# A convolution kernel's reload in four transfers in place of two, one store on ScalarE's queue, and a new order of the work

## The chip, the cores and the metric

The kernel runs on one core of a Trainium2 chip. The metric is the device time of one execution in microseconds (us), the median of several; the profiler records one execution by itself, and its span is the time from the first to the last recorded instruction of that execution. TensorE (PE in the profile) does the matmuls, its weight loads are listed apart (PEld), VectorE is DVE, ScalarE is ACT, GpSimd is POOL, and SyncE (SP) issues DMA transfers. SPq, ACTq and POOLq are the queues by which an engine issues transfers.

## The reference, cut to what matters

x is one sequence of L = 2048 tokens by D = 512 channels in bf16. It is normalised over the channels, and two layers work on the result xn, an S4 convolution with N = 128 modes for each channel, and a gated layer with F = 1792:

```python
P = exp(dt * A)[:, :, None] ** l            # 512 channels, 128 modes, 2048 lags
K = einsum("dn,dnl,dn->dl", C, P, dt * B).real
y = irfft(rfft(pad(xn)) * rfft(pad(K))) + xn * Dskip      # causal convolution over 2048 tokens
h = sigmoid(xn @ w_gate) * (xn @ w_up)
out = x + y + h @ w_down
```

## The kernel before, in words

The kernel is a list of 930 operations, put on the list by `pl.add` and `pl.copy` (lines 258 to 299), each with its engine, what it depends on, and the buffers that it takes and gives back. The table `ORDER` (line 207) is a permutation of that list; `run` (line 291) walks along it, hands out buffers by it, and issues each operation on its engine. An engine does its operations in that order and waits where an operation isn't ready. So the table alone sets what stands behind what on every engine and queue; there are no due times.

There are four strands of work.

- LayerNorm (lines 529 to 590): statistics on VectorE (L542, L543), the square root on POOL (L481, L482), the reciprocal (L501) and the scaling on VectorE (L554) or ScalarE, for groups of four tiles of 128 tokens. The normalised tokens go to memory and come back transposed (`xnT`, L581).
- The convolution's kernel. For four blocks c of 128 columns, VectorE raises powers of the modes step by step (L736, L737, L741, L742) with help of ScalarE (L790), into two tables G and H. TensorE multiplies these in two halves of 64 small matmuls on 128x32 tiles (`f_k`, L821). ScalarE evicts each half to `kq_sb` (L288), two stores of 96 KB bring the block to `k_scr` in memory (the helper `dma`, whose transfers are all recorded as L422), and a reload brings two blocks of it back in another layout, as `kT[pc]` with pc = c // 2. Before, one reload of 384 KB does that for a pair of blocks, behind the four stores of both. Then VectorE adds the skip factor Dskip to one row of it (`f_ds`, L842), and POOL copies one value of that row (L844).
- The convolution itself, in two halves p of the channels (p = 0 uses `kT[0]`, blocks 0 and 1; p = 1 uses `kT[1]`, blocks 2 and 3), with eight units u in each half. A unit has: a load of `z_scr` (256 KB); `fm`, four or more small matmuls on 64x64 tiles (L883); the eviction of their result to x (ScalarE, L288); a swap of 32-row groups of x, by four transfers of 64 KB on SP for p = 0 and for units 4, 6 and 7 of p = 1, by four copies of VectorE (L896) for units 0, 1, 2, 3 and 5 of p = 1; `fk`, ten matmuls of `kT[p]` with a constant E (L909), which need `f_ds`; the eviction of that (ScalarE, L288); two products on VectorE (L914, L918), which need both the swap and the eviction; `fv`, sixteen small matmuls on 64x64 tiles (L933); its eviction (ScalarE) and a store of 256 KB to `v_scr`. At the end the result is loaded again, and TensorE brings it back to tokens (L992, L995).
- The gated layer, in four groups (grp) of 512 tokens, with 14 pieces k of F: gate (L1043) and up (L1067) matmuls of 128x128 weights with 512 tokens, a sigmoid on ScalarE (L1055), a copy of up on ScalarE (L1082) and a product on VectorE (L1087), or a product straight from PSUM (L1092); then down (L1121). These matmuls are what fills TensorE between the pieces of the convolution.

TensorE's full matmuls (L909, L1043, L1067, L1121) use the whole 128x128 array; fm, fv and `f_k` cut it in tiles. A run of such matmuls between full ones is called a visit to small tiles below.

The lines that the change touches are the block's end (lines 831 to 844) and `ORDER`.

Of the kernel before, what the change touches and what calls it, by code (L numbers as in the profile page):

```python
# [13 lines left out]
ACT = mybir.ActivationFunctionType  # L14
# [53 lines left out]
KB = 1024  # L68
# [114 lines left out]
def _consts():  # L183
# [135 lines left out]
def kernel(  # L319
# [336 lines left out]
    W_op = []  # L656
# [63 lines left out]
    kT_op = [[], []]  # L720
    k_st = [[], []]
# [26 lines left out]
    for c in range(4):  # L748
# [83 lines left out]
        kq_free = [dma("SP", k_scr[4 * c:4 * c + 4, :, :, cc, :].rearrange("t i h x -> (t i) h x"),  # L832
                       kq[cc:128:2, cc:16:2].rearrange("p h k y -> p h (k y)"), deps=evs, prio=PC, pkt=192)(96 * KB) for cc in range(2)]
        k_st[pc] += kq_free
        if c % 2 == 0:
            continue
        kr = dma("SP", kT[pc].rearrange("p a c k y -> p a (c k y)"), k_scr[8 * pc:8 * pc + 8].rearrange("a i h c x -> (i h) a (c x)"),
                 deps=k_st[pc] + W_op + [o_g], prio=PC, pkt=384)(384 * KB)

        def f_ds(pc=pc):  # L840
            kz = kTv[pc][0:1, :, 0, :]
            V.tensor_tensor(out=kz, in0=kz, in1=dskr[0:1, DW * pc:DW * pc + DW].rearrange("p (a y) -> p a y", y=16), op=ALU.add)  # L842
        kT_op[pc] = [pl.add("DVE", 0.30, f_ds, [kr, l_dk], PC)]
        pl.add("POOL", 0.1, lambda pc=pc: P.tensor_copy(out=hold[:, pc:pc + 1], in_=kTv[pc][0:1, 0, 0, 0:1]), kT_op[pc], PC)  # L844

    table_free = [x for c in kgen for x in kgen[c]]
# [364 lines left out]
```

## Time and profile before

| | us |
|---|---|
| median of three runs | 215.9 |
| lowest and highest run | 215.29 and 217.3 |
| the profiled execution | 215.17 |
| its span | 213.4 |
| TensorE busy in it | 204.0 |
| VectorE busy in it | 191.2 |
| ScalarE busy in it | 176.7 |
| POOL busy in it | 24.9 |

The profiled execution is 1.77 us longer than its span, which is what lies around the first and the last instruction. The granted TensorE clock was 0.996 of full speed. In the trace, the four kernel matmuls begin at about 79.0, 99.5, 128.2 and 154.9 us, the last down projection at 192.09.

In the rows of groups, `out<-in` are the tiles written and read, xN is how often, and the part behind the bar is busy time, mean time of one in ns, then idle time of that engine just before and what ended most of it. In a timeline a row begins with start and length in us.

### The profile page before, as it was taken

To read this page: it belongs to the slowest core of one execution; us is meant where nothing else is said; L and a number is where in the kernel's file an instruction comes from. 1 tells how busy PE (TensorE), PEld (TensorE's weight loads), DVE (VectorE), ACT (ScalarE), POOL (GpSimd) and SP (SyncE) were. 2 spreads that over 40 slices of the span, in tenths; PEclk is the share of its full clock that TensorE was granted. 3 is DMA by queue.
4 is the path that set the end of the run, shared out by engine and by line. 5 is a ranking of instruction groups with operands and counts; after the bars stand their busy time and mean duration, and the time that the engine had idled before them with its cause. 6 is when DMAs were issued, how large, how long until landed. Compare 5 with 4: busy or idle time off the path is not lost.

```text
span 213.4 us, 4894 instructions
## 1 busy us (share of the span) xinstructions
PE 204.0 (96%) x1839; PEld 103.1 (48%) x1864; DVE 191.2 (90%) x406; ACT 176.7 (83%) x284; POOL 24.9 (12%) x40
## 2 busy tenths in 40 slices
PE   7989999999999999999999999999999999999992
PEld 2554444444444444445446465444554646634472
DVE  4799999998999999999999999999986799991493
ACT  4799999999999999988999998979899797891000
POOL 2120003009340000200000002010170200000000
PEclk9999999999999999999999999999999999999998
DMA  5999399136162243693895659768968989888944
GB/s 138 334 383 378 132 219 315 57 102 147 49 129 71 98 128 122 194 252 117 237 262 153 186 137 289 182 154 214 258 175 209 248 277 322 218 257 224 268 178 172
DMA packets 52346, 42.61 MB, mean 200 GB/s; under 512 B 16610, under 2 KB 44515, under 8 KB 52323
## 3 DMA queue, kind: packets, MB, share of 16 engines
q1 hardware_dynamic: 51154, 40.40, 64.8%
q0 software_dynamic: 864, 1.57, 4.5%
q10 hardware_dynamic: 304, 0.33, 0.5%
q8 instruction: 14, 0.23, 0.4%
q14 instruction: 10, 0.07, 0.1%
HBM read 24.99 MB, written 12.85 MB: 177 GB/s over the span
## 4 chain that ended last, share of the span: by engine, by line
DVE 55%; PE 28%; issue 5%; POOL 5%; DMA 4%; ACT 1%; DVEq 0%; ACTq 0%; SPq 0%
PE bank L1121 10%; PE bank L1043 7%; DVE big L737 6%; DVE big L736 5%; DVE stats L542 4%; DVE big L914 4%; PE bank L1067 4%; DVE big L742 3%; PE pair L909 3%; DVE hT_sb L1087 3%; DVE big L741 3%; DVE hT_sb L1092 3%; DVE big L896 3%; DVE big L678 3%; DMA big<-big 3%
## 5 line engine op out<-in xcount | busy, mean ns | idle before, releaser
L288 ACT ACTIVATE big<-pair 128x1024 bf16<-128x1024 f32 x64 | 64.6, 1041 | 5.5 <-PE pair L909 1.9
L1067 PE MATMUL bank<-xnT,wu_sb 128*128 128x512 bf16 x213 | 52.0, 380 | 1.3 <-issue 0.6
L1121 PE MATMUL bank<-wd_sb,hT_sb 128*128 128x512 bf16 (+1 forms) x231 | 50.6, 367 | 0.5 <-issue 0.2
L1043 PE MATMUL bank<-xnT,wg_sb 128*128 128x512 bf16 (+1 forms) x193 | 45.8, 371 | 0.8 <-ACT xnT L572 0.3
L1043 PEld LDWEIGHTS <-wg_sb 128*128 128x128 bf16 x240 | 22.6, 98 | 25.0 <-issue 2.7
L1121 PEld LDWEIGHTS <-hT_sb 128*128 128x128 bf16 x238 | 22.3, 98 | 25.2 <-issue 2.3
L1067 PEld LDWEIGHTS <-wu_sb 128*128 128x128 bf16 x224 | 21.0, 98 | 26.3 <-issue 3.9
L1055 ACT ACTIVATE hT_sb<-bank 128x512 bf16<-128x512 f32 x48 | 27.4, 616 | 0.1
L736 DVE TENSOR_TENSOR big<-big 128x1024 bf16<-128x1024 bf16 (+4 forms) x40 | 26.8, 670 | 0.2
L737 DVE TENSOR_TENSOR big<-big 128x1024 bf16<-128x1024 bf16 (+4 forms) x40 | 26.6, 664 | 0.0
L1082 ACT ACTIVATE us_sb<-bank 128x512 bf16<-128x512 f32 x40 | 24.0, 621 | 1.0 <-DVE hT_sb L1087 0.8
L914 DVE TENSOR_TENSOR big<-big 128x2048 bf16<-128x2048 bf16 x16 | 19.5, 1219 | 1.3 <-ACT big L288 1.3
L909 PE MATMUL pair<-big 128*128 128x256 bf16 x160 | 19.6, 273 | 0.4 <-DVE big L842 0.2
L909 PEld LDWEIGHTS <-big 128*128 128x128 bf16 x160 | 15.4, 98 | 5.3 <-issue 1.1
L741 DVE TENSOR_TENSOR big<-big 128x512 bf16<-128x512 bf16 (+4 forms) x40 | 16.6, 415 | 0.2
L742 DVE TENSOR_TENSOR big<-big 128x512 bf16<-128x512 bf16 (+4 forms) x40 | 16.6, 414 | 0.0
L790 ACT ACTIVATE sq_sb<-big 128x256 bf16<-128x256 bf16 (+2 forms) x20 | 13.4, 668 | 1.8 <-DVE big L742 1.6
L933 PE MATMUL pair<-big 64*64 64x512 bf16 (+1 forms) x256 | 13.3, 328 | 0.3 <-ACT big L288 0.2
L1087 DVE TENSOR_TENSOR hT_sb<-hT_sb,us_sb 128x1024 bf16<-128x1024 bf16 x20 | 13.5, 683 | 0.0
L288 ACT ACTIVATE big<-big 128x256 bf16<-128x256 bf16 x30 | 13.4, 450 | 0.0
L542 DVE BATCH_NORM_STATS2 stats<-big 128x6 f32<-128x512 bf16 x15 | 9.7, 681 | 3.0 <-DMA big<-in_A_u_dram 3.0
L669 ACT ACTIVATE big<-big 128x1024 f32<-128x1024 f32 x11 | 11.9, 1083 | 0.0
(100 smaller groups left out, 228.9 us busy)
## 6 DMA issues: line engine op xcount, KB each, us to landing
big<-c_E SPq DMA_DIRECT2D x13, 320.0 KB, 4.2
z_scr<-big SPq DMA_DIRECT2D x16, 256.0 KB, 4.8
big<-z_scr SPq DMA_DIRECT2D x16, 256.0 KB, 4.1
v_scr<-big SPq DMA_DIRECT2D x16, 256.0 KB, 3.9
big<-big SPq DMA_DIRECT2D x44, 64.0 KB, 3.3
big<-in_A_u_dram SPq DMA_DIRECT2D x4, 512.0 KB, 10.3
wu_sb<-in_B_w_up_dram SPq DMA_DIRECT2D x2, 896.0 KB, 9.7
wd_sb<-in_B_w_down_dram SPq DMA_DIRECT2D x1, 1792.0 KB, 9.8
```

What stands on the lines that cost most here:

```text
L288: nc.scalar.activation(out=get(out), in_=get(in_), func=ACT.Identity)
L736: V.tensor_tensor(out=wide(outp), in0=wide(lo), in1=mre, op=ALU.mult)
L737: V.tensor_tensor(out=wide(tb()), in0=wide(lo), in1=mim, op=ALU.mult)
L741: V.tensor_tensor(out=outp[:, :, 0], in0=outp[:, :, 0], in1=tb()[:, :, 1], op=opr)
L742: V.tensor_tensor(out=outp[:, :, 1], in0=outp[:, :, 1], in1=tb()[:, :, 0], op=opi)
L909: T.matmul(two(sk)[:, o:o + DW], es()[:, g, kt, :], kTv[p][:, :, kt, :], start=kt in (0, NKT - 1), stop=kt >= NKT - 2)
L914: V.tensor_tensor(out=pp().rearrange("p q h m -> p (q h) m"), in0=xx().rearrange("p q h m -> p (q h) m"), in1=kb()[:, 0:2 * DW].unsqueeze( ...
L1043: T.matmul(bank(sl, k % 2)[:, c0:c1], w[:, kt, k * 128:(k + 1) * 128], xnT[:, grp, kt, c0:c1], start=(kt == 0), stop=(kt == KT - 1))
L1055: S.activation(out=hT_sb[:, hs.idx, k % 2, :], in_=bank(sl), func=ACT.Sigmoid)
L1067: T.matmul(bank(sl), wu_sb[:, kt, k * 128:(k + 1) * 128], xnT[:, grp, kt, :], start=(kt == 0), stop=(kt == KT - 1))
L1082: eus.append(pl.add("ACT", 0.48, lambda sl=sl, us=us, kk=kk: S.activation(out=us_sb[:, us.idx, kk % 2, :], in_=bank(sl), func=ACT.Identity ...
L1121: T.matmul(bank(po)[:, 0:c[1] - c[0]], hT_sb[:, hts[k // 2].idx, k % 2, jj * 128:(jj + 1) * 128], wd_sb[:, k, c[0]:c[1]], start=first and ...
```

## The change

It does three things.

1. Each block c issues its own reload, of its half of `kT[pc]` (192 KB), directly behind its own two stores. `f_ds` depends on the last two of them. There are four reloads where there were two, so the list has 932 operations.
2. The second store of the last block (c = 3) goes to ScalarE's queue.
3. `ORDER` is another permutation. No operation but that store changes its engine, and none but the reloads is added or taken away.

```diff
 ORDER = [
-    0, 1, 2, 3, 5, 4, 12, 11, 24, 26, 25, 27, 28, 30, 29, 36, 37, 38, 31, 32, 33, 39, 41, 40, 47, 20, 34, 42, 43, 44,
...
+    0, 1, 2, 3, 5, 4, 12, 11, 24, 26, 25, 27, 28, 30, 29, 36, 37, 38, 31, 32, 33, 39, 41, 40, 47, 20, 34, 42, 43, 44,
...
+    k_ld = []
...
-        kq_free = [dma("SP", k_scr[4 * c:4 * c + 4, :, :, cc, :].rearrange("t i h x -> (t i) h x"),
+        kq_free = [dma("ACT" if cc and c in (3,) else "SP", k_scr[4 * c:4 * c + 4, :, :, cc, :].rearrange("t i h x -> (t i) h x"),
                        kq[cc:128:2, cc:16:2].rearrange("p h k y -> p h (k y)"), deps=evs, prio=PC, pkt=192)(96 * KB) for cc in range(2)]
         k_st[pc] += kq_free
+        half_kT = slice(4 * (c % 2), 4 * (c % 2) + 4)
+        k_ld.append(dma("SP", kT[pc][:, half_kT].rearrange("p a c k y -> p a (c k y)"), k_scr[4 * c:4 * c + 4].rearrange("a i h c x -> (i h) a (c x)"),
+                        deps=kq_free + W_op + [o_g], prio=PC, pkt=384)(192 * KB))
         if c % 2 == 0:
             continue
-        kr = dma("SP", kT[pc].rearrange("p a c k y -> p a (c k y)"), k_scr[8 * pc:8 * pc + 8].rearrange("a i h c x -> (i h) a (c x)"),
-                 deps=k_st[pc] + W_op + [o_g], prio=PC, pkt=384)(384 * KB)
...
-        kT_op[pc] = [pl.add("DVE", 0.30, f_ds, [kr, l_dk], PC)]
+        kT_op[pc] = [pl.add("DVE", 0.30, f_ds, k_ld[-2:] + [l_dk], PC)]
```

Lines below the change are one or two higher in the new kernel (L736 becomes L737, L842 becomes L844, L896 becomes L898, L909 becomes L911, L1087 becomes L1089). What the new order does is seen engine by engine, at three places.

**SP around the last block's stores.** `kq_sb` is the evicted block, `k_scr` the memory that it goes to, `c_S2` and `c_SR` are constants, `z_scr` is the load of a unit, and `big<-big` with 32x1024 is one transfer of a swap. Before:

```order
L422 DMA big<-c_S 128x128
L422 DMA k_scr<-kq_sb 512x1x96 x2
L422 DMA big<-c_SR 128x256
L422 DMA big<-big 32x1024
L422 DMA big<-z_scr 128x4x256
L422 DMA big<-k_scr 128x8x192
```

Now:

```order
L422 DMA k_scr<-kq_sb 512x1x96
L422 DMA big<-c_S 128x128
L422 DMA big<-c_SR 128x256
L422 DMA big<-big 32x1024 x4
L422 DMA big<-k_scr 128x4x192
```

One of the two stores is gone from this queue; the reload of 4x192 values per partition for the last block has four swap transfers (of p = 1, unit 7) between itself and the store, where before a constant, one transfer of a swap and the load of a unit stood there. The reload of block 2, the other half of that pair, stands sixteen rows further up in the queue.

**ScalarE and VectorE behind the last kernel matmul.** On ScalarE `kq_sb` rows are the evictions of the block, rows with 128x2x2x256 are evictions of fm, rows of 128x1024 those of fv or fk, `hT_sb` is a sigmoid, `us_sb` a copy of up. Before:

```order
L288 ACTIVATE kq_sb<-pair_64 128x96x8
L288 ACTIVATE kq_sb<-pair_63 128x96x8
L1055 ACTIVATE hT_sb<-bank_68 128x512
L288 ACTIVATE big<-pair_64 128x2x2x256
L288 ACTIVATE big<-pair_63 128x2x2x256
L1082 ACTIVATE us_sb<-bank_67 128x512
L1055 ACTIVATE hT_sb<-bank_66 128x512
L288 ACTIVATE big<-pair_64 128x2x2x256
L288 ACTIVATE big<-pair_63 128x2x2x256
```

Now:

```order
L288 ACTIVATE kq_sb<-pair_64 128x96x8
L288 ACTIVATE kq_sb<-pair_63 128x96x8
L422 DMA k_scr<-kq_sb 512x1x96
L288 ACTIVATE big<-pair_64 128x2x2x256
L288 ACTIVATE big<-pair_63 128x2x2x256
L288 ACTIVATE big<-pair_64 128x1024
L1057 ACTIVATE hT_sb<-bank_68 128x512
L1057 ACTIVATE hT_sb<-bank_66 128x512
L288 ACTIVATE big<-pair_64 128x1024
L288 ACTIVATE big<-pair_63 128x2x2x256
```

The store stands directly behind the block's eviction, and the evictions of fm (before units 7 and 3, then 2 and 4) are now in the order 7, 4, then that of p = 0's unit 6, two sigmoids, p = 0's unit 7, and then unit 3; unit 2 follows behind one `us_sb` row. On TensorE the small matmuls stand accordingly: before, fm of units 7 and 3, fm of 2 and 4, and fv of p = 0's units 6 and 7 were three visits; now fm of 7 and 4, fv of 6, fm of 3 with fv of 7, and fm of 2 and 1 are four. From there to the end of the convolution there were 8 more visits, and are 9.

On VectorE, from the products of p = 0's last units (2048 elements) to the products of the first unit of p = 1 that is multiplied, unit 7. Before:

```order
L914 TENSOR_TENSOR big<-big 128x2048
L918 TENSOR_TENSOR big<-big 128x1024
L896 COPY big<-big 32x1024 x8
L842 TENSOR_TENSOR big<-big,dskr 1x16x16
L1087 TENSOR_TENSOR hT_sb<-hT_sb,us_sb 128x1024 x2
L914 TENSOR_TENSOR big<-big 128x2048
```

Now:

```order
L920 TENSOR_TENSOR big<-big 128x1024 x2
L1089 TENSOR_TENSOR hT_sb<-hT_sb,us_sb 128x1024
L898 COPY big<-big 32x1024 x4
L844 TENSOR_TENSOR big<-big,dskr 1x16x16
L898 COPY big<-big 32x1024 x4
L1094 TENSOR_TENSOR hT_sb<-hT_sb,bank_67 128x512
L916 TENSOR_TENSOR big<-big 128x2048
```

Before, both swaps by VectorE (units 2 and 3, eight copies) stood ahead of the skip row (`dskr`), and two products of the gated layer behind it. Now one swap stands ahead of it (unit 3) and one behind it (unit 2), with one of the gated layer's products ahead and one behind.

**VectorE at the last LayerNorm group.** L501 is the reciprocal of the square root that POOL works out from the statistics (L543); L736, L737, L741, L742 are steps of the powers, L676 and L678 steps of their start. Before, from seven rows behind the last L543 on:

```order
L736 TENSOR_TENSOR big<-big 128x128x4
L737 TENSOR_TENSOR big<-big 128x512
L741 TENSOR_TENSOR big<-big 128x64x2
L742 TENSOR_TENSOR big<-big 128x64x2
L676 SCALAR_TENSOR_TENSOR big<-big 128x512
L678 TENSOR_TENSOR big<-big 128x512
L741 TENSOR_TENSOR big<-big 128x64x4
L742 TENSOR_TENSOR big<-big 128x64x4
L501 RECIPROCAL ln_ri_f<-ln_sd_b 128x4
```

Now the last L543 stands twenty rows ahead of L501, and the last eleven of these rows are:

```order
L738 TENSOR_TENSOR big<-big 128x2048
L796 TENSOR_TENSOR big<-sq_sb 128x64x6
L797 TENSOR_TENSOR big<-big 128x64x6
L676 SCALAR_TENSOR_TENSOR big<-big 128x512
L678 TENSOR_TENSOR big<-big 128x512
L737 TENSOR_TENSOR big<-big 128x128x14
L738 TENSOR_TENSOR big<-big 128x1792
L661 CAST big<-big 128x512 x2
L1089 TENSOR_TENSOR hT_sb<-hT_sb,us_sb 128x1024
L742 TENSOR_TENSOR big<-big 128x64x14
L743 TENSOR_TENSOR big<-big 128x64x14
L501 RECIPROCAL ln_ri_f<-ln_sd_b 128x4
```

Between the last statistics and the reciprocal there were 14 rows, with sizes of 64 to 512 elements. There are 20 now, and from the first to the last they take in steps of 1024 to 2048 elements.

78 rows, old and new, of the table ORDER are left out of this document.

## The prediction

> **What bounds the kernel now.** I read the page's busy times first, then a table of windows that I cut at the four kernel matmuls and at the last down projection, then the waits of TensorE and VectorE, and last the timeline around the second reload. The first question is whether any engine has room. The columns of the window table are busy time and instruction count of each engine, granted clock, DMA share, GB/s.
>
> ```profile
> PE 204.0 (96%) x1839; PEld 103.1 (48%) x1864; DVE 191.2 (90%) x406; ACT 176.7 (83%) x284; POOL 24.9 (12%) x40
> ```
> ```profile
> 8.69:79.01 70.32, 68.72 (x365) 31.57 (x373) 68.55 (x161) 69.00 (x113) 12.88 (x16) 1.00 0.57 173
> 79.01:154.92 75.91, 75.09 (x849) 38.51 (x861) 75.36 (x164) 69.45 (x120) 4.51 (x10) 1.00 0.75 198
> 154.92:192.09 37.17, 35.77 (x463) 19.86 (x468) 32.40 (x57) 32.91 (x42) 5.23 (x3) 1.00 0.86 243
> 192.09:213.40 21.31, 17.41 (x140) 10.35 (x139) 10.04 (x12) 0.59 (x1) 0.00 (x0) 0.96 0.71 210
> ```
>
> The reader is to see that TensorE is full to within 1.6, 0.8 and 1.4 us in the first three windows, VectorE to within 1.8 and 0.6 us in the first two, and ScalarE to within 1.3 us in the first. So whatever an order does, it can win little: the stretch up to 192.09 has idle TensorE time of 1.60 + 0.82 + 1.40 = 3.8 us in all, and most of that is the price of single instructions, not a wait for somebody. The waits say what is left (engine, line, what it waited for: total, times, longest):
>
> ```profile
> PE bank L1067 <- issue: 0.6, 4, 0.2
> PE pair L1043 <- DVE xnT L574: 0.6, 1, 0.6
> PE pair L821 <- DVE big L286: 0.4, 1, 0.4
> PE pair L909 <- DVE big L842: 0.2, 1, 0.2
> ```
> ```profile
> DVE big L896 <- issue: 2.8, 1, 2.8
> DVE big L914 <- ACT big L288: 1.3, 1, 1.3
> DVE ln_ri_f L501 <- POOL ln_sd_b L482: 1.2, 1, 1.2
> ```
>
> TensorE waits for the skip row (L842), which stands behind the reload, 0.2 us in the whole kernel. That is the wait that an earlier reload could remove from TensorE. The timeline of the second reload tells why it is so small (start, length, engine, what; the bracket is idle time before):
>
> ```profile
> 155.82 1.51 ACT L288 ACTIVATE kq_sb<-pair 128x768 bf16<-128x768 f32 x2
> 157.35 1.25 SPq L422 DMA_DIRECT2D k_scr<-kq_sb  x2
> 157.89 1.94 ACT L288 ACTIVATE big<-pair 128x1024 bf16<-128x1024 f32 x2
> 160.65 1.99 ACT L288 ACTIVATE big<-pair 128x1024 bf16<-128x1024 f32 x2
> 160.68 0.47 SPq L422 DMA_DIRECT2D big<-k_scr  x1
> 161.81 3.44 DVE L896 COPY big<-big 32x1024 bf16<-32x1024 bf16 x8 [2.83 <-issue]
> 165.28 0.28 DVE L842 TENSOR_TENSOR big<-big,dskr 1x256 bf16<-1x256 bf16 x1
> 165.62 2.08 PEld L909 LDWEIGHTS <-big 128*128 128x128 bf16 x20 [0.71 <-DVE big L842]
> 165.62 2.36 PE L909 MATMUL pair<-big 128*128 128x256 bf16 x20 [0.23 <-DVE big L842]
> 168.04 1.23 DVE L914 TENSOR_TENSOR big<-big 128x2048 bf16<-128x2048 bf16 x1 [1.27 <-ACT big L288]
> ```
> ```profile
> k_scr<-kq_sb SPq DMA_DIRECT2D x8, 96.0 KB, 3.1
> big<-k_scr SPq DMA_DIRECT2D x2, 384.0 KB, 3.3
> ```
>
> The reload is issued at 160.68 and lands 3.3 us later (the median of its two; the last column), at about 164.0. The skip row runs at 165.28, directly behind two swaps (L896) that started when ScalarE's eviction for the first of them had ended. The swaps, not the transfer, put the skip row at 165.28; the transfer had some 1.3 us to spare.
>
> **The change, part by part.** All sums are against the profiled execution, 215.17 us for a span of 213.4; it lies 0.73 us under the median of the runs, 215.9.
>
> (1) The reload in four pieces. Two more transfers on SP's queue, each an issue of some 0.5 us by the row at 160.68, and as many bytes as before. SP issues and waits and computes nothing; its order is told in the part on the change. What counts is when the last piece lands. Its issue stands behind four swap transfers of p1,u7, and these wait for ScalarE's eviction of p1,u7. ScalarE comes from the kernel eviction (155.82 + 1.51 = 157.33), issues its store (0.6, from 1.25 for two at 157.35), evicts u7 (1.0, from 1.94 for two at 157.89): 158.9. Four swap issues at 0.6 bring the reload to 161.3. At the old 3.3 us it lands at 164.6; at 3.1 us, the row for the smallest transfer of this buffer, 164.4. Both lie ahead of the skip row as worked out below (166.2), so cost and gain are nothing; the cover is the swap of p1,u3, and with it gone the price would be what the reload is later than before, 0.6 us. From below: if the reload had set the skip row, an earlier landing could give at most the 0.23 us of TensorE's wait at 165.62.
>
> The Trainium skill (DMA: Bandwidth & Descriptors, Anatomy of one DMA — SWDGE (gpsimd) path) speaks against such a split: each transfer pays a fixed part of about 2.0 us besides its bytes at 436 GB/s, so two halves cost one fixed part more. By it two fixed parts more would be 4.0 us if none were covered, and the sum below would be 220.3. The trace agrees on the fixed part, with 3.1 us for 96 KB and 3.3 us for 384 KB, but here it is paid beside other work.
>
> (2) The store on ScalarE: one issue of 0.6 us in the queue of an engine that TensorE and VectorE wait for there. Behind it stand the evictions of p1,u7 and p1,u4. It is on ScalarE's path to the swap, and I carry it in (4), not twice.
>
> (3) The order up to the last kernel matmul (154.92). At each kernel matmul, the same set of operations stands ahead on TensorE and on VectorE as before, but for pieces of 0.6 to 0.9 us: local exchanges. So only waits can go. The largest is this one:
>
> ```profile
> 48.08 0.18 DVE L543 BATCH_NORM_AGGREGATE mvb<-stats 128x2 bf16<-128x6 f32 x1
> 48.35 4.17 POOL L481 TENSOR_SCALAR ln_ve_b<-mvb 128x4 bf16<-128x4 bf16 x1 [13.04 <-DVE mvb L543]
> 52.60 1.04 POOL L482 TENSOR_TENSOR ln_sd_b<-ln_ve_b,half 128x4 bf16<-128x4 bf16 x1
> 53.67 0.18 DVE L501 RECIPROCAL ln_ri_f<-ln_sd_b 128x4 f32<-128x4 bf16 x1 [1.24 <-POOL ln_sd_b L482]
> 54.02 0.68 DVE L736 TENSOR_TENSOR big<-big 128x1024 bf16<-128x1024 bf16 x1
> 79.04 1.42 PE L821 MATMUL pair<-big 128*32 128x82 bf16 x128 [0.36 <-DVE big L286]
> ```
>
> POOL needs 4.17 + 1.04 us between the last statistics (48.08) and the reciprocal (53.67), and VectorE had only 4.2 us of work to put in between. The new order puts twenty rows there, seven of them at 1024 elements or more, each at least 0.68 us by the row at 54.02: 4.8 us, and over 5.2 with the other thirteen, so the 1.24 us go. What of it reaches the end? VectorE's own gain is 0 to 1.24; TensorE, which is as full, had waited 0.36 us on VectorE at 79.04, and gets no more than that back at this place. I take -0.4, TensorE's row, since TensorE is the fuller of the two up to the end (ends: -1.2 and 0; and up to +0.8 if the exchanges make as much new idle time as TensorE has now between 79.01 and 154.92).
>
> (4) The order after 154.92. Two durations per operation are needed: ScalarE's, and what TensorE pays for the small-tile matmuls (L883, L933), given by the window 154.92 to 192.09:
>
> ```profile
> L288 ACT ACTIVATE big<-pair 128x1024 bf16<-128x1024 f32 x64 | 64.6, 1041 | 5.5 <-PE pair L909 1.9
> L1055 ACT ACTIVATE hT_sb<-bank 128x512 bf16<-128x512 f32 x48 | 27.4, 616 | 0.1
> L1082 ACT ACTIVATE us_sb<-bank 128x512 bf16<-128x512 f32 x40 | 24.0, 621 | 1.0 <-DVE hT_sb L1087 0.8
> L883 PEld LDWEIGHTS <-m 64*64 64x64 bf16 x28 | 0.8, 104 | 1.8 <-issue 1.7
> ```
> ```profile
> 157.29 0.20 PEld L883 LDWEIGHTS <-m 64*64 64x64 bf16 x8 [0.42 <-issue]
> 157.85 1.04 PE L1067 MATMUL bank<-xnT,wu_sb 128*128 128x512 bf16 x4
> ```
>
> Whenever TensorE goes from full tiles to small ones its weight load stands idle 0.42 us with nobody to wait for (the row at 157.29), and the window's row for L883 has 1.7 us of that. On the way back its matmuls show no gap (157.85). So I take 0.4 us for each visit to small tiles. Counting the order, there were 11 visits after the last kernel matmul and there are 13 now: fm of p1,u2 and u4, and fv of p0,u6 and u7, no longer go together. That is +0.8 us for TensorE, 0.4 of it ahead of fk of p1,u7.
>
> The other path: ScalarE after 157.33 now issues the store (0.6), evicts p1,u7 and p1,u4 (2 x 1.0), p0,u6 (1.04), two sigmoids (2 x 0.62), p0,u7 (1.04), and then p1,u3 (1.0): 164.2. The swap of u3 follows at half of 3.44, to 165.9, the skip row to 166.2, so fk of p1,u7 starts at 166.2 instead of 165.62: +0.6. TensorE gets there by itself at 165.62 - 0.23 + 0.4 for the visit + 0.3 for fm of p1,u1 that now stands ahead: 166.1. The two agree. Then fk of p1,u7, its eviction and its product (L914) all come 0.6 us later than 168.04, and from there VectorE has next to no gap: of its 4.8 us of idle time in the window (37.17 - 32.40) 2.83 + 1.27 lie ahead of L914. So +0.6 is kept on VectorE. On TensorE the visits make +0.8. They lie beside each other, and the larger counts: +0.8. Ends: 0, if the visits fall into idle time that is there anyway (1.40 us in that window), and +1.5, if both add.
>
> (5) The tail after 192.09 has the same operations, with t0 and t1, t2 and t3 exchanged: nothing, and what hides it is that all of them are needed before the last store; bound 0 to +0.4 by the same visit price.
>
> Sum: 0 + 0 - 0.4 + 0.8 + 0 = +0.4. Profiled 215.17 + 0.4 = 215.6; against the median 215.9, **216.3 us**.
>
> **Rivals.** A: slower, by ScalarE. The swap of p1,u3, and with it the skip row, now hangs on seven evictions and an issue in a row instead of five rows of work. I let ScalarE run without a gap for 6.9 us, and it has gaps: in the window from 154.92 it is busy 32.91 of 37.17 us. If the eviction of p1,u3 slips by as much as VectorE's wait in front of L896 is now (2.83), the end comes 2.8 us later, since VectorE has no gap behind L914: 216.3 + 2.8 = 219.1. It decides from the point at which fk of p1,u7 starts after 167.8 (2.2 us later than now). For it: ScalarE's queue is in order, and one late fv holds all behind it. Against: TensorE reaches fm of p1,u3 at about 161.9 by its own row of groups, 1.3 us ahead of when I let ScalarE take it.
>
> B: faster, by waits. The 1.24 us at L501 reach the end in full, and the extra visits lie in idle time, while the 0.71 us of weight-load wait at 165.62 goes too: -1.24 - 0.71 - 0.36 = -2.3, 213.6. For it: VectorE is as full as TensorE up to 154.92. Against: TensorE is idle 0.82 us in the whole of 79.01 to 154.92, so 1.24 us can't come through there.
>
> C: the reload did hold the kernel. Then its earlier, smaller transfer gives back VectorE's 2.83 us at 161.81: 215.9 - 2.8 = 213.1. Against: the wait ends with ScalarE's eviction, and the reload's issue moves from 160.68 to 161.3, which is later. So here the change doesn't do what it says.
>
> The Trainium skill (DMA: Bandwidth & Descriptors, Issuing engines are not separate DMA queues) says that issuing from a second engine saves the issue time alone. That would leave 0.6 us on SP's queue, and no run here shows more yet.
>
> **How the numbers follow.** Likeliest, no change beyond what a measurement of this kernel can tell (about 1%, 2.2 us): 0.46, for which 214.0 to 218.0 is its own range. A, and other waits of its kind that a whole new order may open: 0.32. B: 0.18. C: 0.04. Faster by over 1% means under 213.7, slower over 218.1. The range goes from 213.2, which is B's end and nearly C's, to 220.0, a little behind A's price.
>
> **What would show it.** Right, if VectorE's wait at L501 is gone and TensorE's at L821 with L286 shrinks; if the skip row (now L844) starts between 165.5 and 167 on the old scale, behind a swap and not behind a DMA; if weight loads of L885 and L935 idle 0.42 us at two places more; and if four transfers of 192 KB stand in the list of issues, at about 3.2 us each. Wrong, if the skip row waits for a transfer (then (1) failed), if VectorE's wait ahead of L898 grows beyond 5 us (A), or if TensorE shows a wait of over 1 us that before has not, at a place other than these: then the exchanges that I called local were not.

## The result, and the profile after

The changed kernel took 215.05 us, median of 20 runs (214.32 to 215.93), against 215.94 for the kernel before (20 runs, 214.62 to 217.33). The ratio that the measurement gives is 0.9947, with a 95% interval from 0.993 to 0.9964; the two medians alone give 0.9959. It is a gain of about half a per cent, some 0.9 to 1.1 us, where 0.4 us more had been forecast. Two later measurements of the same kernel gave 0.9974 (0.9951 to 0.9997) and 0.9951 (0.9925 to 0.9977). Executions more than 1.5% above the fastest of their kernel are left out of every comparison.

The profiled execution took 215.32 us and has a span of 213.4 us, as long as that of before: a single execution of either kernel varies by more than the difference, so a comparison of the two pages alone would have shown nothing. It is read stretch by stretch. First the windows of the changed kernel, cut at the same events as before:

```profile
8.69:77.97 69.28, 68.06 (x365) 31.34 (x371) 68.73 (x161) 68.23 (x113) 11.41 (x16) 1.00 0.58 173
77.97:154.02 76.05, 75.10 (x850) 38.48 (x860) 75.46 (x163) 70.48 (x122) 18.90 (x12) 1.00 0.74 197
154.02:191.51 37.49, 36.07 (x463) 19.86 (x468) 32.06 (x55) 32.14 (x40) 0.43 (x1) 1.00 0.84 241
191.51:213.40 21.89, 17.49 (x140) 10.36 (x139) 10.34 (x13) 0.59 (x1) 0.00 (x0) 0.97 0.71 214
```

The first stretch is 1.04 us shorter than before (69.28 against 70.32), the next is 0.14 longer, the third 0.32 longer, the tail 0.58 longer. So the order ahead of the first kernel matmul gained about 1 us, and this execution gave it all back in the three stretches behind. The waits say where it was given back; first those of VectorE, then those of TensorE:

```profile
DVE big L898 <- issue: 4.4, 1, 4.4
DVE ln_ri_f L493 <- POOL ln_sd_b L492: 0.7, 1, 0.7
DVE big L844 <- DMA big<-k_scr: 0.5, 1, 0.5
```
```profile
PE pair L1045 <- DVE xnT L574: 0.8, 1, 0.8
PE pair L994 <- DMA big<-v_scr: 0.5, 1, 0.5
PE pair L911 <- DVE big L844: 0.4, 1, 0.4
```

The wait at L501 is gone, and so is that of the kernel matmul for L286. Two new ones have a DMA as their releaser: the skip row (L844) waits for the reload, and the tail's matmuls (L994) wait for the load of `v_scr`. The timeline of the reload, which answers to that of before:

```profile
155.02 1.51 ACT L288 ACTIVATE kq_sb<-pair 128x768 bf16<-128x768 f32 x2 [0.53 <-PE pair L822]
156.56 0.64 ACTq L422 DMA_DIRECT2D k_scr<-kq_sb  x1
156.63 0.57 SPq L422 DMA_DIRECT2D k_scr<-kq_sb  x1
158.44 3.68 SPq L422 DMA_DIRECT2D big<-big  x4
162.74 0.38 SPq L422 DMA_DIRECT2D big<-k_scr  x1
163.27 1.71 DVE L898 COPY big<-big 32x1024 bf16<-32x1024 bf16 x4 [4.37 <-issue]
165.49 0.28 DVE L844 TENSOR_TENSOR big<-big,dskr 1x256 bf16<-1x256 bf16 x1 [0.51 <-DMA big<-k_scr]
165.82 2.36 PE L911 MATMUL pair<-big 128*128 128x256 bf16 x20 [0.35 <-DVE big L844]
168.18 1.23 DVE L916 TENSOR_TENSOR big<-big 128x2048 bf16<-128x2048 bf16 x1
```

And the chain of waits at that place (start, length, what), then the landing times:

```profile
156.56 6.16 DMA k_scr<-kq_sb
162.74 2.72 DMA big<-k_scr
165.82 2.36 PE pair L911 x20
```
```profile
big<-k_scr SPq DMA_DIRECT2D x4, 192.0 KB, 5.0
k_scr<-kq_sb SPq DMA_DIRECT2D x7, 96.0 KB, 3.3
```

The reader is to see that store and reload are now on the chain. The last store holds it for 6.2 us, the reload for 2.7, and the skip row starts when the reload has landed, 0.5 us after the swap is done. The four swap transfers ahead of the reload were issued by 162.12 (158.44 + 3.68); the reload went at 162.74, when the stores had landed.

### The profile page after: what moved, and what is told of

Read it like the earlier page. It is cut to its first block, busy times and chain, and to the rows that moved or that the text cites. A ratio compares the mean times of both kernels' runs of the same rounds, so it can differ in the third digit from the quotient of the medians.

```text
span 213.4 us, 4897 instructions
## 1 busy us (share of the span) xinstructions
PE 204.0 (96%) x1839; PEld 103.2 (48%) x1864; DVE 191.3 (90%) x406; ACT 176.3 (83%) x284; POOL 33.1 (15%) x40
## 4 chain that ended last, share of the span: by engine, by line
PE 59%; ACT 20%; DMA 9%; DVE 6%; issue 4%; POOL 1%; DVEq 0%; ACTq 0%; SPq 0%
PE bank L1069 15%; PE bank L1123 13%; PE bank L1045 11%; PE pair L911 9%; ACT big L288 6%; PE pair L935 5%; ACT hT_sb L1057 3%; PE pair L1045 3%; DMA k_scr<-kq_sb 3%; ACT us_sb L1084 3%; ACT big L669 3%; ACT big L663 2%; DVE big L1020 2%; DMA big<-v_scr 2%; PE pair L822 2%
## 5 line engine op out<-in xcount | busy, mean ns | idle before, releaser
L1069 PE MATMUL bank<-xnT,wu_sb 128*128 128x512 bf16 x212 | 53.0, 379 | 1.1 <-issue 0.6
L1045 PE MATMUL bank<-xnT,wg_sb 128*128 128x512 bf16 (+1 forms) x194 | 46.6, 370 | 0.5 <-issue 0.3
L1057 ACT ACTIVATE hT_sb<-bank 128x512 bf16<-128x512 f32 x48 | 28.7, 640 | 2.3 <-PE bank L1045 2.3
L737 DVE TENSOR_TENSOR big<-big 128x1024 bf16<-128x1024 bf16 (+4 forms) x40 | 26.8, 670 | 0.2
L1084 ACT ACTIVATE us_sb<-bank 128x512 bf16<-128x512 f32 x40 | 24.7, 640 | 0.0
L911 PE MATMUL pair<-big 128*128 128x256 bf16 x160 | 19.4, 273 | 0.4 <-DVE big L844 0.4
L846 POOL COPY hold<-big 1x1 bf16<-1x1 bf16 x2 | 14.3, 7146 | 30.7 <-DVE big L844 30.7
L911 PEld LDWEIGHTS <-big 128*128 128x128 bf16 x160 | 15.3, 98 | 4.8 <-issue 1.0
L742 DVE TENSOR_TENSOR big<-big 128x512 bf16<-128x512 bf16 (+4 forms) x40 | 16.6, 415 | 0.3
L791 ACT ACTIVATE sq_sb<-big 128x256 bf16<-128x256 bf16 (+2 forms) x20 | 14.0, 698 | 1.3 <-DVE big L743 1.0
L1089 DVE TENSOR_TENSOR hT_sb<-hT_sb,us_sb 128x1024 bf16<-128x1024 bf16 x20 | 13.5, 684 | 0.0
L669 ACT ACTIVATE big<-big 128x1024 f32<-128x1024 f32 x11 | 12.4, 1125 | 0.4 <-DVE big L678 0.4
```

The source lines that it names most:

```text
L669: s_op = pl.add("ACT", 0.95, lambda cur=cur, sq=sq: S.activation(out=sq, in_=cur, func=ACT.Square), [cur_op] + W_op[-1:], PLAD + k * 0.01)
L737: V.tensor_tensor(out=wide(outp), in0=wide(lo), in1=mre, op=ALU.mult)
L911: T.matmul(two(sk)[:, o:o + DW], es()[:, g, kt, :], kTv[p][:, :, kt, :], start=kt in (0, NKT - 1), stop=kt >= NKT - 2)
L1045: T.matmul(bank(sl, k % 2)[:, c0:c1], w[:, kt, k * 128:(k + 1) * 128], xnT[:, grp, kt, c0:c1], start=(kt == 0), stop=(kt == KT - 1))
L1057: S.activation(out=hT_sb[:, hs.idx, k % 2, :], in_=bank(sl), func=ACT.Sigmoid)
L1069: T.matmul(bank(sl), wu_sb[:, kt, k * 128:(k + 1) * 128], xnT[:, grp, kt, :], start=(kt == 0), stop=(kt == KT - 1))
```

## The experiments

The rows of each run were put together in one table. The columns are: VectorE's wait at the last group's L501; the time from the first of the three L501 (18.4 to 18.8 us) to the first kernel matmul; from the last kernel matmul to the product L914 of p = 1, unit 7; from there to the last down projection; from there to the last add (L1141). From the first kernel matmul to the last it was 75.9 to 76.2 us in every run. All are differences of two starts in the timeline of the run's profile. The wait of e11_recip_early is 0.93 us at L501 and 0.99 us at the row behind it. "Ahead" and "behind" mean the order up to the last kernel matmul and that after it.

| run | wait | to first kernel matmul | to L914 | to down | to last add | ratio to before |
|---|---|---|---|---|---|---|
| before | 1.24 | 60.55 | 13.12 | 24.05 | 17.65 | |
| e6_before, a second profile | 0.93 | 60.23 | 13.30 | 24.06 | 18.57 | |
| e3_split | 0 | 59.59 | 13.11 | 24.06 | 18.17 | 1.0003 (0.9981 to 1.0025) |
| e2_back | 0.93 | 60.22 | 13.86 | 23.48 | 17.66 | 1.0002 (0.998 to 1.0023) |
| e4_recip | 0 | 59.59 | 13.50 | 24.06 | 18.46 | 0.9991 (0.9971 to 1.0011) |
| e17_recip, the same | 0 | 59.61 | 13.82 | 24.05 | 17.65 | 0.9978 (0.9953 to 1.0004) |
| e12_min | 0 | 59.61 | 13.12 | 24.22 | 17.65 | 0.9989 (0.9965 to 1.0012) |
| e14_min, the same | 0 | 59.59 | 13.15 | 24.05 | 17.65 | 0.9961 (0.9935 to 0.9987) |
| e1_front | 0 | 59.40 | 14.74 | 24.05 | 17.66 | 0.9995 (0.9977 to 1.0014) |
| e7_front_split | 0 | 59.38 | 13.72 | 24.76 | 18.42 | 1.002 (0.9993 to 1.0047) |
| e9_nosplit | 0 | 59.39 | 13.63 | 23.33 | 19.24 | 1.0008 (0.9986 to 1.0029) |
| e16_nosplit, the same | 0 | 59.38 | 14.21 | 23.33 | 19.34 | 0.9989 (0.9965 to 1.0013) |
| after | 0 | 59.38 | 14.16 | 23.33 | 18.32 | 0.9947 (0.993 to 0.9964) |
| e5_after, the same | 0 | 59.38 | 13.54 | 23.33 | 18.00 | 0.9974 (0.9951 to 0.9997) |
| e15_after, the same | 0 | 59.39 | 13.64 | 23.58 | 17.98 | 0.9951 (0.9925 to 0.9977) |
| e10_sp_store | 0 | 59.43 | 14.26 | 23.30 | 18.31 | 0.9977 (0.9951 to 1.0004) |
| e13_loads_behind | 0 | 59.39 | 13.83 | 23.40 | 17.65 | 0.996 (0.9936 to 0.9984) |
| e11_recip_early | 1.92 | 60.95 | 14.24 | 23.33 | 18.04 | 1.0076 (1.0049 to 1.0103) |

**The two halves of the order.** e1_front takes the new order up to the last kernel matmul and the old one behind it, in the kernel before; e2_back is the changed kernel with the two the other way round.

```python
X = new[:new.index(last_kernel_matmul) + 1]
e1_front = X + [n for n in old if n not in X]
```

> The kernel before with the new order up to the last kernel matmul only, and its old order behind it; two reloads, all stores on SP. Theory F (the gain is made ahead of the first kernel matmul, by the wait at L501 that is gone, and is kept): the first kernel matmul starts about 1.0 us earlier than in the kernel before (78.0), the last one at about 154.0, and the median is 0.8 to 1.2 us lower. Rival S (the gain comes from the split reload and the store on ScalarE): within 0.3 us of before. Rival B (it comes from the order behind the last kernel matmul): within 0.3 us of before.

> The changed kernel with the old order up to the last kernel matmul: split reload, store on ScalarE, new order behind it. Theory F: no gain, 0 to +0.7 us against before, the last part being no better than it was. Rivals S and B: 0.8 to 1.2 us lower than before.

Neither half moved the time: 0.9995 and 1.0002. For e2_back that is what theory F expected. For e1_front it was right on the milestone (last kernel matmul at 153.86) and wrong on the end. The timeline shows the place where it was lost:

```profile
160.90 3.44 DVE L897 COPY big<-big 32x1024 bf16<-32x1024 bf16 x8 [2.77 <-issue]
161.72 0.38 SPq L423 DMA_DIRECT2D big<-k_scr  x1
165.84 0.28 DVE L843 TENSOR_TENSOR big<-big,dskr 1x256 bf16<-1x256 bf16 x1 [1.50 <-DMA big<-k_scr]
```

VectorE finished its swaps early and then waited 1.50 us for the reload of 384 KB. Part (1) of the forecast had priced a reload without its cover, at 0.6 us, and taken it for covered. A new theory D followed: a gain ahead is kept only if the reload lets it through.

**The split alone.** e3_split puts two reloads of 192 KB in the place of each of 384 KB.

> The kernel before with each 384 KB reload issued as two of 192 KB, one behind the other at the old place; order and queues else unchanged. Theory F: within 0.3 us of before, since the reload is covered by the swaps. Rival S: 0.5 us or more lower; a fixed cost per transfer on the path would make it 0.6 us or more higher.

1.0003: alone it changes nothing, as the forecast had it. (In the profile of this run POOL happened to be quick, so VectorE did not wait at L501; the last section comes back to that.)

**The wait alone.** e4_recip moves one operation of the kernel before.

```python
order.remove(136); order.insert(order.index(137), 136)   # 136: L501, 137: the first scaling L554 behind it
```

> The kernel before with one operation moved: the reciprocal L501 of the last LayerNorm group stands behind the next step of the powers (L736, L737) instead of ahead of it. Theory F, if the wait of 1.24 us at L501 is what was lost: VectorE's wait there is 0 to 0.2 us, the first kernel matmul starts 0.8 to 1.2 us earlier, and the median is 0.8 to 1.2 us lower. Rival, the forecast's own reckoning: TensorE gets back only its 0.36 us. Rival, another step of the order ahead makes the gain: within 0.2 us of before.

The wait was 0, and the column to the first kernel matmul says what that is worth: 59.6 us without a wait, 60.2 with 0.93, 60.55 with 1.24. So 0.63 of 0.93 us and 0.96 of 1.24 came through to TensorE, where the forecast let 0.36 through. The time hardly moved (0.9991, then 0.9978 in e17_recip, which came out between the two ranges expected for it). Part of the gain went again at the reload, here in the second of these runs, whose stretch to L914 is 0.6 us longer than the mean of before (13.82 against 13.21):

> The kernel before with the reciprocal one step later and nothing else, again. If the wait at L501 alone makes the gain: 0.3 to 0.5% below before, as with the two small edits together. If the shorter reload is needed to keep it: within 0.2% of before, and VectorE waits 0.3 us or more for big<-k_scr.

```profile
160.55 0.47 SPq L423 DMA_DIRECT2D big<-k_scr  x1
161.20 3.44 DVE L897 COPY big<-big 32x1024 bf16<-32x1024 bf16 x8 [2.82 <-issue]
165.35 0.28 DVE L843 TENSOR_TENSOR big<-big,dskr 1x256 bf16<-1x256 bf16 x1 [0.70 <-DMA big<-k_scr]
```

**Both small edits.** e12_min and e14_min are the kernel before with the moved reciprocal and the reloads of 192 KB, the early halves issued ahead of the next block's store (block 0) and ahead of a store of `v_scr` (block 2), all stores on SP.

> The kernel before with two edits alone: the reciprocal L501 one step later, and reloads of 192 KB, each issued when its block is stored. Order else unchanged, all stores on SP. Theory D (a wait that is gone ahead, and a reload short enough not to take the gain back): 0.3 to 0.5% below before. Rival O (the order behind the last kernel matmul is needed too): within 0.2% of before.

> The kernel with the two small edits again (reciprocal one step later, 192 KB reloads), beside the changed kernel on one chip. Theory D: 0.3 to 0.5% below before and within 0.2% of the changed kernel. Rival O: 0.3% or more above the changed kernel.

The first run came out at 0.9989, in the range of rival O, the second at 0.9961, in that of theory D, beside the changed kernel's 0.9951 on one chip. On average these two edits gain 0.25%, in the old order, and the three measurements of the changed kernel 0.43%: more than half of the gain, as far as these intervals can tell. That the split adds to the moved reciprocal isn't shown by the times (that one alone has 0.09 and 0.22%). What shows it is the skip row, which in both profiles follows the swaps with no bracket, where e4_recip and e17_recip had waited 0.47 and 0.70 us; here in e14_min:

```profile
160.46 0.47 SPq L424 DMA_DIRECT2D big<-k_scr  x1
161.30 3.44 DVE L900 COPY big<-big 32x1024 bf16<-32x1024 bf16 x8 [2.82 <-issue]
164.76 0.28 DVE L846 TENSOR_TENSOR big<-big,dskr 1x256 bf16<-1x256 bf16 x1
```

The reload is issued at the same time as there (160.46 against 160.55), with the last half of the bytes, and lands at least 0.5 us sooner.

**The new order without the split, and the new order ahead with it.** e9_nosplit is the changed order with reloads of 384 KB; e7_front_split is e1_front with those of 192 KB.

> The changed kernel's order and its store on ScalarE, but reloads of 384 KB, two in all, at the place of the second of each pair. Theory D with the split as what lets the gain through: VectorE waits 1 us or more for big<-k_scr, and the median is within 0.4 us of before. Rival O: 0.7 us or more below before, like the changed kernel.

> The changed order and the store on ScalarE with two reloads of 384 KB, again. If the split is needed in the changed kernel: within 0.2% of before again, with a wait of VectorE for big<-k_scr or a longer wait of TensorE for big<-v_scr. If the first run of it met a late load of v_scr by chance: 0.3% or more below before.

> The new order up to the last kernel matmul with the four 192 KB reloads, the old order behind it, all stores on SP. Theory D with the split as what lets the gain through: VectorE's wait for big<-k_scr, 1.5 us with one reload of 384 KB, is under 0.5 us, and the median is 0.7 to 1.2 us below before. Rival O (the order behind the last kernel matmul is needed for it): within 0.4 us of before, as with the unsplit reload.

Without the split the gain is gone, twice (1.0008, 0.9989). But theory D had the place wrong: VectorE waited for the reload 0 us in e9_nosplit, where 1 us or more was expected, and 0.6 us in e16_nosplit. In both profiles the gain is lost mostly in the tail, at the load of `v_scr`, here in e16_nosplit:

```profile
PE pair L993 <- DMA big<-v_scr: 1.5, 1, 1.5
```

It was 1.4 us in e9_nosplit, against 0.5 and 0.2 in two profiles of the changed kernel and no such row in the third. On the chain of waits that load takes 5.4 and 5.5 us without the split, and 4.6, 4.1 and 4.3 in the changed kernel. Why a larger reload at 161 us should make a load at 194 us late isn't settled, and two profiles don't show that it does. e7_front_split missed theory D: the wait for the reload fell from 1.5 to 0.5 us, but 0.7 us came up behind L914 and the time was that of before. Joining two orders makes waits of its own, so the hybrids bound nothing by themselves.

**The wait put back, and the store.** e11_recip_early moves the statistics' square root, mean and reciprocal up in the changed kernel; e10_sp_store issues all stores on SP.

```diff
-        kq_free = [dma("ACT" if cc and c in (3,) else "SP",
+        kq_free = [dma("SP",
```

> The changed kernel with the square root and the reciprocal of the last LayerNorm group moved up again, the reciprocal about 2.4 us of VectorE work behind the statistics in place of 12. Theory F: VectorE waits there some 1 us (the square root takes POOL 1.9 us and more), the first kernel matmul comes 0.6 to 1.0 us later than in the changed kernel, and the median is within 0.2% of before. Rival (the gain ahead is made by other steps of the order): still 0.3% or more below before.

> The changed kernel with all stores on SP, order as changed. Theory D (front gain kept only where the split reload and the order behind it let it through; the store on ScalarE is a detail): 0.3 to 0.6% below before, like the changed kernel. Rival S (the store on ScalarE is needed, since it lets both stores start together): within 0.2% of before, and VectorE waits 0.6 us longer at the skip row.

VectorE now waited twice, for POOL's root and for ScalarE's mean:

```profile
DVE ln_nb_f L504 <- ACT ln_m_f L498: 1.0, 1, 1.0
DVE ln_ri_f L503 <- POOL ln_sd_b L484: 0.9, 1, 0.9
```

1.9 us of waiting put the first kernel matmul 1.6 us later and the end with it: 217.19 us, 1.0076, which is 2.2 us above e10_sp_store, measured beside it. That is more than expected, since a second wait came with it and VectorE then waited 0.7 us for the reload as well. It is the clearest sign that a wait of VectorE in this stretch reaches the end. The store on ScalarE made no difference that these runs can tell: with all stores on SP the ratio is 0.9977, between the two ranges expected, and VectorE waited 0.7 us at the skip row, against 0.5, 0 and 0 in the changed kernel.

**The changed kernel again, and two loads behind the store.** e6_before and e5_after are second profiles. e13_loads_behind issues two loads of `z_scr` behind the last store instead of ahead of it.

> The kernel before, for a second profile of it. Theory D: the first kernel matmul starts within 0.7 us of 79.0, the wait for big<-k_scr or for big<-v_scr differs from the first profile by 0.3 us or more. Rival (the two profiles differ by their orders alone): the same milestones within 0.2 us.

> The changed kernel once more, on the chip that times the three others. All theories: 0.7 to 1.4 us below before. Theory D (two loads that the chain waits for, the second reload and the load of v_scr, land at times that vary from run to run, and eat a gain of the order ahead): the last kernel matmul starts near 154.0 again, and the waits of VectorE for big<-k_scr and of TensorE for big<-v_scr come out otherwise than 0.5 and 0.5 us, anywhere from 0 to 1.5.

> The changed kernel again, for the comparison with the two others: 0.3 to 0.6% below before by all theories.

> The changed kernel with two loads of z_scr (256 KB each, units 2 and 1 of the second half) issued behind the last block's store instead of ahead of it. Theory D, that in the changed kernel the last third hangs on store and reload, which queue behind those loads: the last store lands about 3.5 us after its issue instead of 5 to 6, the wait of VectorE for big<-k_scr is 0, the skip row comes 0.3 to 0.5 us earlier after the last kernel matmul, and the median is 0 to 0.4 us below that of the changed kernel. Rival (fm of units 2 and 1 now waits for its loads): the skip row no earlier, and 0.5 us or more above the changed kernel.

e5_after came out 0.6 us below before (0.9974), a little short of its range, and e15_after within its own (0.9951). The two profiles of before differ as theory D has it, by 0.3 us at L501, and by 0.9 us in the tail, with a wait that the first had not:

```profile
PE pair L992 <- DMA big<-v_scr: 0.7, 1, 0.7
```

e13_loads_behind came out at 0.996, no better than the changed kernel. Its reload was still issued 5.6 us after the last store (156.31 to 161.94) and VectorE waited 0.3 us for it, so those two loads alone are not what makes the reload late.

## Why the prediction was wrong, point by point

Two steps of the forecast failed. Term (3), the order ahead, was mis-sized: -0.4 us forecast, some -0.8 to -1.0 measured. Term (4), +0.8 us for the order behind, did not come: from the last kernel matmul to the last down projection the mean is 37.2 us in the changed kernel and 37.3 before. So the sum had the wrong sign.

**Sum.** The means of the three profiles of the changed kernel against the two of before: to the first kernel matmul -1.0 us (59.38 against 60.39), to the last +0.1, to L914 +0.6 (13.78 against 13.21), to the down projection -0.6 (23.41 against 24.06), tail 0.0. That is -0.9, and the medians differ by -0.89. The forecast had -0.4, 0, +0.6, 0.2 on top of that, and 0. The first term depends on how long VectorE waits at L501, which varies: with e2_back and e3_split, whose order ahead is that of before, the four profiles have waits of 1.24, 0.93, 0.93 and 0 us and a mean of 60.15, and the term is -0.8.

**(3), the order ahead: mis-sized, and the larger error.** The wait at L501 went, as forecast. The forecast then let only TensorE's own 0.36 us at the kernel matmul through. What comes through is most of VectorE's wait: 0.96 of 1.24 us by the table, 1.6 of 1.9 in e11_recip_early. A view that the forecast did not use says so for the kernel before: its chain of waits runs over POOL's two instructions and then over VectorE all the way to that matmul (start, length, what; most rows left out):

```profile
48.35 4.18 POOL ln_ve_b L481
52.60 1.05 POOL ln_sd_b L482
75.12 0.69 DVE big L678
75.81 0.60 DVE big L736
76.41 0.60 DVE big L737
78.10 0.60 DVE hT_sb L1087
79.04 1.42 PE pair L821 x115
```

From the first L501 to the first kernel matmul VectorE is busy 59.1 to 59.2 us in before, e6_before, e3_split and the changed kernel alike, and the stretch takes 60.6, 60.3, 59.6 and 59.4 us: VectorE's idle time makes the difference. TensorE's idle time at one matmul is no cap on what an earlier VectorE gives it: over the whole stretch TensorE's idle time fell from 1.60 to 1.22 us (69.28 - 68.06), and its busy time, whose ends are modelled, from 68.72 to 68.06. The other exchanges ahead are worth 0.2 us (59.38 against 59.6).

**(4), behind the last kernel matmul: half right.** L914 was to come 0.6 us later, and did on average (13.78 against 13.21). That the mean agrees is partly luck: the three profiles give 0.95, 0.33 and 0.43, and the first has in it the wait of 0.5 us for the reload, which (1) had ruled out. "So +0.6 is kept on VectorE" failed: all of it was made up before the down projection. So did the 0.8 us for two more visits to small tiles. The weight loads' idle time ahead of small tiles, before and then in the changed kernel, each in its stretch from the last kernel matmul to the last down projection:

```profile
L933 PEld LDWEIGHTS <-big 64*64 64x64 bf16 x160 | 4.1, 106 | 5.0 <-issue 1.6 <-DVE big L918 1.1 <-DVE rz L955 0.4
```
```profile
L935 PEld LDWEIGHTS <-big 64*64 64x64 bf16 x160 | 4.2, 106 | 4.6 <-issue 1.6 <-DVE big L920 1.1
L885 PEld LDWEIGHTS <-m 64*64 64x64 bf16 x28 | 0.8, 103 | 2.3 <-issue 1.3 <-DMA v_scr<-big 0.4 <-DMA big<-c_E 0.4
```

With L883's 1.8 it was 6.8 us, and it is 6.9 now. Two visits more should have made 0.8. The idle time of fm's loads grew by 0.5, and that of fv's fell by 0.4. Between L914 and the down projection TensorE's idle time halved. Before and now:

```profile
168.04:192.09 24.05, 23.19 (x240) 12.77 (x242) 23.50 (x40) 20.92 (x25) 0.00 (x0) 1.00 0.91 265
```
```profile
168.18:191.51 23.33, 22.91 (x236) 12.53 (x238) 23.02 (x40) 20.48 (x25) 0.00 (x0) 1.00 0.88 264
```

It was 0.86 us and is 0.42, with VectorE at 23.02 of 23.33 us. VectorE also has 0.5 us less work there (23.02 against 23.50), and TensorE four matmuls less: the new order has that work further ahead. So the +0.6 ahead of L914 and the -0.6 behind it are in part one exchange across that product, which the forecast did not count. e2_back, with the old order ahead, takes 23.48 us there as well, so it belongs to the order behind. Which exchange does it was not tried.

**(1), the reload: right alone, wrong in company.** "Cost and gain are nothing" holds for the order of before (e3_split, 1.0003). But the 1.3 us to spare were no margin: the reload and its store land at times that vary. On the chain of waits the reload of 384 KB took 4.5 us in the second profile of before, where 3.3 had been reckoned with; VectorE waited 0.2 us for it there, and 0.5 and 0.7 us once it was early (e4_recip, e17_recip). The forecast also had the four swap issues set the reload's place, and no term for the stores' landing, which set it in the first profile of the changed kernel. By e3_split the split alone is worth nothing; by e9_nosplit and e16_nosplit the changed kernel has no gain without it. How it keeps the gain is shown in part only: at the skip row in the old order, but in the new order the loss came up in the tail. The forecast's test for this step, a skip row that waits for a transfer, came true in the changed kernel too (0.5, 0 and 0 us in its three profiles). The rule of the Trainium skill on a transfer's fixed part (DMA: Bandwidth & Descriptors, Anatomy of one DMA — SWDGE (gpsimd) path), which spoke against the split, did not decide: the transfer that is waited for became shorter, and the added ones lie beside other work. The section's 2.0 us are a fit for transfers that GpSimd issues; these are issued by SP. The medians of before, 3.1 us for 96 KB and 3.3 us for 384 KB, put the part that doesn't grow with the size at about 3.0 us (an estimate), so the trace agrees that there is such a part, but not on its size.

**(2), the store on ScalarE:** nothing, within what these runs tell. **(5), the tail:** its length is 17.65 us plus a wait for the load of `v_scr`, 0 to 1.7 us from run to run; the exchanged tiles show no cost.

Rival A did not happen (fk of unit 7 at 165.82, where it needed 167.8), nor did rival C: VectorE's wait ahead of the swap grew, to 4.4 us. Rival B named the right cause, the wait at L501, and was put at -2.3 by counting TensorE's 0.36 on top of the wait that makes it, and the 0.71 us at fk of unit 7, which stayed. What the forecast held against it, that 79.01 to 154.92 has no room for 1.24 us, was no objection: that stretch did not get shorter, it only began and ended earlier.

## What to carry to other kernels

In this kernel two engines were both full, and a wait on one of them in front of a common event was worth most of its length up to that event; the other engine's idle time there was no cap on it. A transfer that lands shortly before it is needed is covered only as long as nothing ahead gets faster: ask of each gain which hidden transfer is next, and make that one short in the same change. When the effect is smaller than the scatter of one execution, compare stretches between events over several profiles; the totals of two profiles say nothing here. And when work is moved across the event at which a stretch is cut, read the stretches on both sides together.

## What was not expected of the hardware

The same two POOL instructions of the square root took 4.17 + 1.04 us in the kernel before, 1.22 + 3.68 us in its second profile, and 0.57 + 1.33 us in the changed kernel. With one and the same order, e3_split had no wait at L501 where e2_back had 0.93, since the second of them took 1.85 us in one and 3.67 us in the other:

```profile
50.02 1.85 POOL L484 TENSOR_TENSOR ln_sd_b<-ln_ve_b,half 128x4 bf16<-128x4 bf16 x1
52.71 0.18 DVE L503 RECIPROCAL ln_ri_f<-ln_sd_b 128x4 f32<-128x4 bf16 x1
```
```profile
49.65 3.67 POOL L484 TENSOR_TENSOR ln_sd_b<-ln_ve_b,half 128x4 bf16<-128x4 bf16 x1
53.35 0.18 DVE L503 RECIPROCAL ln_ri_f<-ln_sd_b 128x4 f32<-128x4 bf16 x1 [0.93 <-POOL ln_sd_b L484]
```

So part of the scatter of the kernel before came from POOL, and an order that puts 12 us of other work in between takes it out.
